# One score tile of four banks for two key chunks, one exponential for both, and the products of a group placed side by side on TensorE

## The chip, the cores and the metric

The kernel runs on one core of one Trainium2 chip. The time is device microseconds of one execution. Of the kernel before, three runs were timed and one further execution was recorded by the hardware profiler. All rows below come from that one.

## What is computed

Routed attention, then a feed-forward block with squared ReLU:

```python
# q, k, v: (4, 8, 768, 64); centroids: (8, 16, 64); w_in: (512, 2048); w_out: (2048, 512)
q_assign = argmax(einsum('bhsd,hcd->bhsc', q_n, c_n), axis=-1)   # nearest of 16 centroids
k_assign = argmax(einsum('bhsd,hcd->bhsc', k_n, c_n), axis=-1)
mask = q_assign[:, :, :, None] == k_assign[:, :, None, :]
scores = where(mask, q @ k.T / sqrt(64), -1e9)
attn = softmax(scores)
x = (attn @ v) as (3072, 512)
h = x @ w_in                                       # (3072, 2048)
out = (maximum(h, 0) ** 2) @ w_out                 # (3072, 512)
```

## The kernel before

**Units.** Two heads make a pair (16 pairs, 4 per batch). The 768 queries of a pair are two halves of 384. The 768 keys are six chunks of 128. The main loop (L481) goes over units `(pair, half, c)` of two key chunks: three units make a half, 96 units in all, numbered from 0. Units 0 to 11 are the first halves of batch 0, units 12 to 23 its second halves, and from unit 24 on both halves of a pair follow each other.

**Scores.** `scores` (L329) handles one chunk. Keys are the stationary operand, so a tile `sc` holds 128 keys by 384 queries for each of the two heads, in one bank per head. Head 0 lies on rows 0 to 63 of the contraction, head 1 on rows 64 to 127, so the products of the two heads use different halves of TensorE's rows. In batch 0 the mask is added by two further products of one-hot codes (L340, "oh"). In the later batches the exponentials are masked on VectorE (L347), by a comparison of the query's and the key's cluster ids. ScalarE takes the exponential of each chunk (L345, 768 elements in each partition). GpSimd adds up the exponentials of a half (`acc`, L357 and L361), except in the first halves of batch 0, where TensorE sums them (`sm`, L374).

**Values.** Two units later (`LAG`), `times_v` (L363) multiplies the exponentials with V: head 0 writes the upper 64 partitions of `av`, head 1 the lower 64, so here the two heads use different halves of TensorE's columns. At the end of a half, `finish` sums `acc` over the partitions with two products (`sm`, L393), takes a reciprocal (`rb`, L397) and writes the scaled result to `xT` (L398).

**Other work on TensorE.** `prep` makes a pair ready: transposes of q and k (`pt`, L229), logits against the centroids (`lg`, L245), their transposes (`lt`, L256). VectorE finds the ids from them (L260 to L281). From batch 1 on six id products in two tiles spread the ids over the partitions (`pb`, L305). A finished batch or half gives FFN work: 64 products `ph` of 384 columns and 48 products `po` of 512 for each half (L416, L429); they are handed out to the units in equal shares as `fill`. On the chip each float32 product of these kinds stands in the trace as two records.

**Start.** The 32 blocks of the weights come in as 64-bit numbers and are rounded, two for each unit: two steps on ScalarE (L131, L133), three on VectorE (L136, L140, L143), one on GpSimd (L147).

**Order.** No order is written out by hand. A list scheduler places the instructions of each engine: of those that are ready by its own estimate it takes the one with the highest priority, and priority falls in the order in which the program is written. Each engine then runs its own list in order. So a score product can be placed alone where its tile is free and its partner's is not, or where something of higher priority is ready in between. PSUM's eight banks are: two tiles of two for scores (`ps_sc`, L71), two for `av` and the first sums, two for all else (`ps_f`). The exponentials have seven tiles of one chunk each (`expp`, L60).

Of the kernel before, what the change touches and what calls it, by code (L numbers as in the profile page):

```python
# [8 lines left out]
F32 = mybir.dt.float32  # L9
# [15 lines left out]
def kernel(  # L25
# [10 lines left out]
    nc = tc.nc  # L36

    B, H, S, D = q.shape
    C = centroids.shape[1]
    NCH = S // P  # L40
# [39 lines left out]
    raw_v = {}  # L80
# [78 lines left out]
    ups = const.tile([P, D], F32, name="ups")  # L159
# [12 lines left out]
    cnT = const.tile([P, H * C], F32, name="cnT")  # L172
# [46 lines left out]
    qkT = {}  # L219
    ids = {}  # L220
    qid = {}
# [19 lines left out]
    def logits(pair):  # L241
        hp = pair % HP
        lg = bank("lg", [P, TB])
        for g in range(4):
            nc.tensor.matmul(  # L245
                lg[32 * g : 32 * g + 32], lhsT=cnT[:, 2 * C * hp : 2 * C * (hp + 1)],
                rhs=qkT[pair][:, NB * g : NB * (g + 1)], start=True, stop=True,
            )
        lgs[pair] = rbp.tile([P, TB], F32, name="lgs", tag="rb")
        nc.scalar.copy(out=lgs[pair], in_=lg)  # L250

# [67 lines left out]
    ex = {}  # L319
    acc = {}  # L320
    sums = {}

    def first_half(pair, h):
        return pair < HP and h == 0

    av = {}
    xT = {}

    def scores(pair, h, c):  # L329
        sc = ps_sc.tile([P, 2, 512], F32, name="sc")  # L330
        for e in range(2):
            rows = slice(D * e, D * (e + 1))
            nc.tensor.matmul(  # L333
                sc[:, e, 0:TB], lhsT=qkT[pair][rows, NCH + c],
                rhs=qkT[pair][rows, NB * h : NB * (h + 1)], start=True, stop=pair >= HP,
            )
        if pair < HP:
            for e in range(2):
                rows = slice(D * e, D * (e + 1))
                nc.tensor.matmul(  # L340
                    sc[:, e, 0:TB], lhsT=qid[pair][1][rows, 1, c * P : (c + 1) * P],
                    rhs=qid[pair][1][rows, 0, h * TB : (h + 1) * TB], start=False, stop=True,
                )
        t = expp.tile([P, 2, TB], F32, name="ex")
        nc.scalar.activation(out=t, in_=sc[:, :, 0:TB], func=ACT.Exp, scale=SCALE)  # L345
        for e in range(0 if pair < HP else 2):
            nc.vector.scalar_tensor_tensor(  # L347
                out=t[:, e], in0=qid[pair][1][:, h, e],
                scalar=ids[pair][:, c % NB, 2 + c // NB, e : e + 1], in1=t[:, e],
                op0=ALU.is_equal, op1=ALU.mult,  # L350
            )
        ex[pair, h, c] = t
        if first_half(pair, h):
            return
        if c == 1:
            acc[pair, h] = accp.tile([P, 2, TB], F32, name="acc")
            nc.gpsimd.tensor_tensor(  # L357
                out=acc[pair, h], in0=ex[pair, h, 0], in1=t, op=ALU.add
            )
        elif c > 1:  # L360
            nc.gpsimd.tensor_tensor(out=acc[pair, h], in0=acc[pair, h], in1=t, op=ALU.add)  # L361

    def times_v(pair, h, c):  # L363
        if c == 0:
            av[pair, h] = ps_av.tile([P, TB], F32, name="av", tag="av")
            if first_half(pair, h):
                sums[pair, h] = ps_av.tile([P, TB], F32, name="sm", tag="av")
        for e in range(2):
            nc.tensor.matmul(  # L369
                av[pair, h][D * e : D * (e + 1)], lhsT=raw_v[pair][:, e, c],  # L370
                rhs=ex[pair, h, c][:, e], start=(c == 0), stop=(c == NCH - 1),
            )
        for e in range(2 if first_half(pair, h) else 0):
            nc.tensor.matmul(  # L374
                sums[pair, h][D * e : D * (e + 1)], lhsT=ups, rhs=ex[pair, h, c][:, e],
                start=(c == 0), stop=(c == NCH - 1),
            )
        if c > 0:
            ex.pop((pair, h, c))
            ex.pop((pair, h, 0), None)  # L380

    def finish(pair, h):
        b, hp = divmod(pair, HP)
        if hp == 0:
            pool = xtp if (2 * b + h) % 3 < 2 else later["xT"]
            xT[b, h] = pool.tile([P, KT, TB], F32, name="xT")
        if first_half(pair, h):
            sm = sums.pop((pair, h))
        else:
            total = acc.pop((pair, h))  # L390
            sm = bank("sm", [P, TB])
            for e in range(2):
                nc.tensor.matmul(  # L393
                    sm[D * e : D * (e + 1)], lhsT=ups, rhs=total[:, e], start=True, stop=True
                )
# [85 lines left out]
    for u in range(len(units) + LAG):  # L481
        if u < len(units):
            pair, h, c = units[u]
            if (p := next_pair(u)) is not None:
                ahead.extend(prep(p))
            if c == 0 and u + 3 < len(units) and units[u + 3][0] not in raw_v:
                load_v(units[u + 3][0])
            for i in range(2):
                scores(pair, h, c + i)
        done = None  # L490
        if u >= LAG:
            pair, h, c = units[u - LAG]
            for i in range(2):
                times_v(pair, h, c + i)
# [241 lines left out]
```

## Time and profile before

| What | us |
|---|---|
| median of three runs (lowest, highest) | 1160.06 (1159.22, 1162.47) |
| profiled execution | 1158.28 |
| its span, first to last instruction | 1156.4 |
| TensorE busy (matmuls) | 1112.3 |
| VectorE busy | 552.3 |
| ScalarE busy | 316.4 |
| GpSimd busy | 312.8 |

How to read it: the span is 1.9 us shorter than the time of the same execution; what lies outside is not in the trace. A busy time is the time in which at least one instruction ran on an engine. Matmuls overlap, so a busy TensorE can still be slowed by the way in which they follow each other. The page also has a chain of waits: from the last instruction back, at each step to what released it. Where it stays on TensorE, its pieces are the net time that each group of matmuls cost, from its start to the start of the next.

### The profile page before, as it was taken

How to read it: one execution, taken by the hardware profiler on the slowest of the kernel's cores; microseconds unless marked ns; L12 is line 12 of the kernel's file. 1: busy time of each engine (PE TensorE's matmuls, PEld its weight loads, DVE VectorE, ACT ScalarE, POOL GpSimd, SP SyncE). 2: the span in 40 equal slices, each digit the busy share in tenths (PEclk: the TensorE clock that was granted, in tenths of full speed). 3: DMA queues.
4: the chain of work that ended last, by engine and by line, in shares of the span. 5: the costliest groups of instructions: out<-in, count | busy, mean ns of one | idle time of the engine just before them, and what ended most of it. 6: DMA issues, size and time to landing. Idle time of an engine off the chain costs nothing.

```text
span 1156.4 us, 10628 instructions
## 1 busy us (share of the span) xinstructions
PE 1112.3 (96%) x4195; PEld 511.6 (44%) x4195; DVE 552.3 (48%) x762; ACT 316.4 (27%) x512; POOL 312.8 (27%) x181
## 2 busy tenths in 40 slices
PE   5987999999999999999999999999999998999997
PEld 3432444444444434544445444544444443554543
DVE  5999222238676665752456533664455641210200
ACT  4765322223332323221223312232122210110110
POOL 2445422214343333331223231331232321000000
PEclk8998999999999999999999999999999999999999
DMA  8864001120110101010100102000000000000000
GB/s 212 257 201 147 15 13 33 31 60 1 41 38 4 50 10 50 1 41 10 45 15 9 34 9 60 1 14 1 18 24 1 1 10 18 1 1 19 9 10 20
DMA packets 63883, 44.32 MB, mean 38 GB/s; under 512 B 51537, under 2 KB 56657, under 8 KB 63825
## 3 DMA queue, kind: packets, MB, share of 16 engines
q1 hardware_dynamic: 63824, 43.56, 13.2%
q8 instruction: 35, 0.57, 0.2%
q14 instruction: 24, 0.19, 0.1%
HBM read 37.26 MB, written 6.29 MB: 38 GB/s over the span
## 4 chain that ended last, share of the span: by engine, by line
PE 88%; DVE 7%; issue 2%; ACT 1%; DMA 1%; SPq 1%; POOL 0%; DVEq 0%; POOLq 0%; ACTq 0%
PE ph L416 30%; PE po L429 29%; PE sc L333 11%; PE av L369 11%; PE sm L393 2%; PE pt L229 2%; DVE w_raw L143 1%; PE pb L305 1%; DVE rb L397 1%; PE lg L245 1%; DVE w_in L136 1%; DVE ids L271 1%; DVE best L266 1%; DVE mx L260 1%; DVE best L262 1%
## 5 line engine op out<-in xcount | busy, mean ns | idle before, releaser
L416 PE MATMUL ph<-xT,w_in 128*128 128x384 f32 x1024 | 353.3, 495 | 0.0
L429 PE MATMUL po<-w_out,gT 128*128 128x512 f32 x768 | 347.9, 599 | 0.0
L361 POOL TENSOR_TENSOR acc<-acc,ex 128x768 f32<-128x768 f32 x112 | 215.0, 1919 | 399.0 <-DVE ex L347 322.7
L347 DVE SCALAR_TENSOR_TENSOR ex<-qid,ids,ex 128x384 f32<-128x384 bf16 x288 | 229.3, 847 | 158.1 <-ACT ex L345 157.8
L416 PEld LDWEIGHTS ph<-xT,w_in 128*128 128x128 f32 x1024 | 188.3, 190 | 153.3 <-issue 26.7
L429 PEld LDWEIGHTS po<-w_out,gT 128*128 128x128 f32 x768 | 139.8, 190 | 174.5 <-issue 171.1
L345 ACT ACTIVATE ex<-sc 128x768 f32<-128x768 f32 x192 | 149.1, 809 | 209.2 <-PE sc L333 153.0
L424 DVE TENSOR_TENSOR gT<-gT 128x384 f32<-128x384 f32 x128 | 91.8, 721 | 221.1 <-ACT gT L423 220.8
L333 PE MATMUL sc<-qkT 64*128 64x384 f32 x768 | 185.2, 518 | 2.1 <-ACT ex L345 2.1
L369 PE MATMUL av<-ex,v_raw 128*64 128x384 f32 x768 | 156.3, 504 | 7.5 <-DVE rb L397 7.5
L423 ACT ACTIVATE gT<-ph 128x384 f32<-128x384 f32 x128 | 62.9, 491 | 290.2 <-PE ph L416 290.2
L397 DVE RECIPROCAL rb<-sm 128x384 f32<-128x384 f32 x32 | 81.7, 2554 | 87.0 <-PE sm L393 81.1
L333 PEld LDWEIGHTS sc<-qkT 64*128 64x128 f32 x768 | 74.0, 188 | 88.3 <-issue 60.1
L357 POOL TENSOR_TENSOR acc<-ex 128x768 f32<-128x768 f32 x28 | 50.7, 1811 | 179.2 <-DVE ex L347 153.2
L369 PEld LDWEIGHTS av<-ex,v_raw 128*64 128x64 f32 x768 | 49.1, 137 | 94.1 <-issue 83.6
L436 ACT COPY osb<-po 128x512 f32<-128x512 f32 x24 | 14.1, 586 | 175.5 <-PE po L429 175.5
L147 POOL TENSOR_TENSOR w_in<-w_in,w_raw 128x512 int32<-128x512 int32 x16 | 22.7, 1418 | 42.6 <-DVE w_raw L143 39.7
L234 ACT COPY qkT<-pt 128x512 f32<-128x512 f32 x32 | 18.7, 584 | 53.4 <-PE pt L229 53.4
L309 ACT CAST qid<-pb 128x384 bf16<-128x384 f32 x48 | 21.9, 480 | 40.2 <-PE pb L305 40.0
L143 DVE SCALAR_TENSOR_TENSOR w_raw<-w_raw 128x512 uint32<-128x512 uint32 x32 | 30.6, 955 | 0.5 <-ACT w_raw L133 0.5
L232 DVE COPY qkT<-pt 128x512 f32<-128x512 f32 x16 | 11.0, 689 | 40.2 <-PE pt L229 40.2
L147 POOL TENSOR_TENSOR w_out<-w_out,w_raw 128x512 int32<-128x512 int32 x16 | 22.3, 1392 | 24.3 <-DVE w_raw L143 17.7
(72 smaller groups left out, 396.1 us busy)
## 6 DMA issues: line engine op xcount, KB each, us to landing
w_raw<-in_moe_w_in_dram SPq DMA_DIRECT2D x16, 512.0 KB, 5.5
w_raw<-in_moe_w_out_dram SPq DMA_DIRECT2D x16, 512.0 KB, 3.5
v_raw<-in_v_dram SPq DMA_DIRECT2D x20, 384.0 KB, 3.3
q_raw<-in_q_dram SPq DMA_DIRECT2D x32, 192.0 KB, 3.8
k_raw<-in_k_dram SPq DMA_DIRECT2D x32, 192.0 KB, 4.0
out_dram<-osb SPq DMA_DIRECT2D x24, 256.0 KB, 2.0
cen<-in_centroids_dram SPq DMA_DIRECT2D x1, 32.0 KB, 1.9
```

Of the source, the lines that this page charges most:

```text
L147: nc.gpsimd.tensor_tensor(out=dst, in0=dst, in1=lo, op=ALU.add)
L333: nc.tensor.matmul(sc[:, e, 0:TB], lhsT=qkT[pair][rows, NCH + c], rhs=qkT[pair][rows, NB * h : NB * (h + 1)], start=True, stop=pair >= HP,)
L345: nc.scalar.activation(out=t, in_=sc[:, :, 0:TB], func=ACT.Exp, scale=SCALE)
L347: nc.vector.scalar_tensor_tensor(out=t[:, e], in0=qid[pair][1][:, h, e], scalar=ids[pair][:, c % NB, 2 + c // NB, e : e + 1], in1=t[:, e], ...
L357: nc.gpsimd.tensor_tensor(out=acc[pair, h], in0=ex[pair, h, 0], in1=t, op=ALU.add)
L361: nc.gpsimd.tensor_tensor(out=acc[pair, h], in0=acc[pair, h], in1=t, op=ALU.add)
L369: nc.tensor.matmul(av[pair, h][D * e : D * (e + 1)], lhsT=raw_v[pair][:, e, c], rhs=ex[pair, h, c][:, e], start=(c == 0), stop=(c == NCH - 1),
L397: nc.vector.reciprocal(out=rb, in_=sm)
L416: nc.tensor.matmul(ph, lhsT=w_in[:, kk, f * P : (f + 1) * P], rhs=xT[b, h][:, kk], start=(kk == 0), stop=(kk == KT - 1),)
L423: nc.scalar.activation(out=gT[f], in_=ph, func=ACT.Relu)
L424: nc.vector.tensor_tensor(out=gT[f], in0=gT[f], in1=gT[f], op=ALU.mult)
L429: nc.tensor.matmul(po, lhsT=gT[f][:, i * P : (i + 1) * P], rhs=w_out[:, f], start=(f == 0), stop=(f == FT - 1),)
```

## The change

- A unit's two chunks go into one tile of four banks, `[P, 2, 2, 512]` (chunk, head, 512). There is one such tile (`ps_sc`, `bufs=1`) where there were two of two banks.
- One exponential covers both chunks: 1536 elements in each partition instead of two of 768. `expp` has three tiles of two chunks instead of seven of one.
- A new helper, `together`, writes the first product of a group at its usual priority and the others at one raised by 2000, so that the scheduler puts them right behind the first. It is used for logits, scores (with the one-hot products behind them), values with the first sums, and the sums of a half.
- The masks and the sums on GpSimd are the same instructions on slices of the new tile.

```diff
-    expp = ctx.enter_context(tc.tile_pool(name="expp", bufs=7))
+    expp = ctx.enter_context(tc.tile_pool(name="expp", bufs=3))
-    ps_sc = ctx.enter_context(tc.tile_pool(name="ps_sc", bufs=2, space=PSUM))
+    ps_sc = ctx.enter_context(tc.tile_pool(name="ps_sc", bufs=1, space=PSUM))
+    def together(products):
+        products = iter(products)
+        nc.tensor.matmul(**next(products))
+        with tc.high_priority(offset=2000):
+            for product in products:
+                nc.tensor.matmul(**product)
 def scores(pair, h, c):
-        sc = ps_sc.tile([P, 2, 512], F32, name="sc")
+        sc = ps_sc.tile([P, 2, 2, 512], F32, name="sc")
+        heads = [(i, e, slice(D * e, D * (e + 1))) for i in range(2) for e in range(2)]
+        products = [
+            dict(
+                out=sc[:, i, e, 0:TB], lhsT=qkT[pair][rows, NCH + c + i],
                 rhs=qkT[pair][rows, NB * h : NB * (h + 1)], start=True, stop=pair >= HP,
             )
+            for i, e, rows in heads
+        ]
         if pair < HP:
+            products += [
+                ...
+            ]
+        together(products)
-        t = expp.tile([P, 2, TB], F32, name="ex")
-        nc.scalar.activation(out=t, in_=sc[:, :, 0:TB], func=ACT.Exp, scale=SCALE)
+        t = expp.tile([P, 4, TB], F32, name="ex")
+        nc.scalar.activation(
+            out=t, in_=sc.rearrange("p i e n -> p (i e) n")[:, :, 0:TB], func=ACT.Exp, scale=SCALE
+        )
 ...
 def times_v(pair, h, c):
-        for e in range(2):
-            nc.tensor.matmul(
-                av[pair, h][D * e : D * (e + 1)], lhsT=raw_v[pair][:, e, c],
-                rhs=ex[pair, h, c][:, e], start=(c == 0), stop=(c == NCH - 1),
-            )
+        for what in ["av", "sums"] if first_half(pair, h) else ["av"]:
+            for i in range(2):
+                for e in range(2):
+                    products.append(dict(
+                        out=(av if what == "av" else sums)[pair, h][D * e : D * (e + 1)],
+                        lhsT=raw_v[pair][:, e, c + i] if what == "av" else ups,
+                        rhs=t[:, 2 * i + e], start=(c + i == 0), stop=(c + i == NCH - 1),
+                    ))
+        together(products)
```

**TensorE, where a pair is routed (the last one, pair 15).** Before, from the transposes of its logits on (`lt`; `sc` scores, `av` values, `pb` id products, `ph` FFN products, `sm` sums; "..." where rows are left out):

```order
L256 MATMUL lt<-ident,lgs 128x128 x3
L333 MATMUL sc<-qkT 128x384 x4
L369 MATMUL av<-ex,v_raw 64x384
...
L416 MATMUL ph<-xT,w_in 128x384 x4
L333 MATMUL sc<-qkT 128x384
...
L305 MATMUL pb<-ident_b,ids_b 128x128
L333 MATMUL sc<-qkT 128x384
L416 MATMUL ph<-xT,w_in 128x384 x5
L333 MATMUL sc<-qkT 128x384 x2
L369 MATMUL av<-ex,v_raw 64x384 x4
```

Here the four score products of a unit stand at three places, and the values of an earlier one are cut by the id products too. After, at the same place (L81 is the first product of a group, L84 are the others):

```order
L266 MATMUL lt<-ident,lgs 128x128 x3
L81 MATMUL sc<-qkT 128x384
L84 MATMUL sc<-qkT 128x384 x3
L81 MATMUL av<-ex,v_raw 64x384
L84 MATMUL av<-ex,v_raw 64x384 x3
...
L315 MATMUL pb<-ident_b,ids_b 128x128
L81 MATMUL sc<-qkT 128x384
L84 MATMUL sc<-qkT 128x384 x3
L435 MATMUL ph<-xT,w_in 128x384 x4
```

Every group is whole, and between two score groups stand four value products and six id products.

**ScalarE, at the end of the rounding of the weights.** Before, from the two steps of the 30th weight to the first ReLU (`gT`); an exponential is half a unit: the two single rows are unit 11, x6 are units 12 to 14:

```order
L131 ACTIVATE w_out<-w_raw 128x512
L133 ACTIVATE w_raw<-w_raw 128x512
L345 ACTIVATE ex<-sc 128x768
L131 ACTIVATE w_out<-w_raw 128x512
L133 ACTIVATE w_raw<-w_raw 128x512
L345 ACTIVATE ex<-sc 128x768
L131 ACTIVATE w_out<-w_raw 128x512
L133 ACTIVATE w_raw<-w_raw 128x512
L345 ACTIVATE ex<-sc 128x768 x6
L423 ACTIVATE gT<-ph 128x384 x2
```

After, an exponential is a whole unit; the first row is unit 10's, x3 are units 11 to 13, and the weights between are the 30th to 32nd:

```order
L360 ACTIVATE ex<-sc 128x1536
L139 ACTIVATE w_out<-w_raw 128x512
L141 ACTIVATE w_raw<-w_raw 128x512
L139 ACTIVATE w_out<-w_raw 128x512
L141 ACTIVATE w_raw<-w_raw 128x512
L139 ACTIVATE w_out<-w_raw 128x512
L141 ACTIVATE w_raw<-w_raw 128x512
L360 ACTIVATE ex<-sc 128x1536 x3
L442 ACTIVATE gT<-ph 128x384
```

Unit 11's exponential has moved behind the last weight's steps, and single ReLUs now stand between the units that follow.

## Rows read from the trace of the kernel before

**Rows 1.** Page, head: span, and each engine's busy time and instructions.
```profile
span 1156.4 us, 10628 instructions
PE 1112.3 (96%) x4195; PEld 511.6 (44%) x4195; DVE 552.3 (48%) x762; ACT 316.4 (27%) x512; POOL 312.8 (27%) x181
```

**Rows 2.** Busy time by stretch: length, five engines (count), granted clock, DMA share, GB/s.
```profile
13.70:111.00 97.30, 77.58 (x429) 35.05 (x430) 90.90 (x133) 63.89 (x101) 42.28 (x31) 0.88 0.70 213
123.30:979.80 856.50, 850.31 (x3226) 382.75 (x3224) 429.19 (x566) 223.81 (x360) 258.24 (x136) 1.00 0.08 21
```

**Rows 3.** Waits of matmuls, 123 to 980 us: total us, times, longest.
```profile
PE pb L305 <- DVE ids_b L281: 6.1, 10, 0.8
```

**Rows 4.** Chain of waits, undisturbed units: start us, net us, what (records).
```profile
879.97 1.49 PE sc L333 x8
881.46 1.44 PE av L369 x8
882.90 6.00 PE ph L416 x18
888.90 0.80 PE sm L393 x4
```

**Rows 5.** Chain of waits where pair 15 is routed.
```profile
863.36 2.78 PE ph L416 x8
866.14 0.84 PE sc L333 x2
866.98 0.44 PE pb L305 x6
867.42 0.84 PE sc L333 x2
868.26 3.42 PE ph L416 x10
871.68 0.85 PE sc L333 x4
```

**Rows 6.** Groups of ScalarE (busy, mean ns | idle), then a timeline of one unit.
```profile
L345 ACT ACTIVATE ex<-sc 128x768 f32<-128x768 f32 x192 | 149.1, 809 | 209.2 <-PE sc L333 153.0 <-PE sc L340 30.0 <-issue 24.6
L309 ACT CAST qid<-pb 128x384 bf16<-128x384 f32 x48 | 21.9, 480 | 40.2 <-PE pb L305 40.0
...
416.93 1.51 ACT L345 ACTIVATE ex<-sc 128x768 f32<-128x768 f32 x2 [0.32 <-PE sc L333]
...
415.92 1.56 PE L333 MATMUL sc<-qkT 64*128 64x384 f32 x8
```

**Rows 7.** Timeline: the last weight's steps on ScalarE and VectorE.
```profile
106.81 0.67 ACT L133 ACTIVATE w_raw<-w_raw 128x512 f32<-128x512 uint32 x1
...
112.86 0.42 DVE L140 TENSOR_SCALAR w_out<-w_out 128x512 uint32<-128x512 uint32 x1
```

**Rows 8.** Chain of waits, end of the start stage.
```profile
97.64 0.68 DVE w_raw L143
...
100.02 0.68 DVE w_raw L143
...
114.61 0.85 PE sc L333 x4
115.46 0.16 PE sc L340 x2
115.62 0.65 PE sc L333 x4
116.26 0.16 PE sc L340 x2
...
119.21 2.57 DVE rb L397
...
129.98 0.84 PE sc L333 x4
```

**Rows 9.** Waits of matmuls for exponentials, whole span: total us, times, longest.
```profile
PE sc L333 <- ACT ex L345: 2.1, 2, 1.1
```

More of the change, by code (lines that the diff above doesn't have):

```diff
@@ L243, in logits @@
         lg = bank("lg", [P, TB])
-        for g in range(4):
-            nc.tensor.matmul(
-                lg[32 * g : 32 * g + 32], lhsT=cnT[:, 2 * C * hp : 2 * C * (hp + 1)],
+        together(
+            dict(
+                out=lg[32 * g : 32 * g + 32], lhsT=cnT[:, 2 * C * hp : 2 * C * (hp + 1)],
                 rhs=qkT[pair][:, NB * g : NB * (g + 1)], start=True, stop=True,
             )
+            for g in range(4)
+        )
         lgs[pair] = rbp.tile([P, TB], F32, name="lgs", tag="rb")
@@ L329, in scores @@
     def scores(pair, h, c):
-        sc = ps_sc.tile([P, 2, 512], F32, name="sc")
-        for e in range(2):
-            rows = slice(D * e, D * (e + 1))
-            nc.tensor.matmul(
-                sc[:, e, 0:TB], lhsT=qkT[pair][rows, NCH + c],
+        sc = ps_sc.tile([P, 2, 2, 512], F32, name="sc")
+        heads = [(i, e, slice(D * e, D * (e + 1))) for i in range(2) for e in range(2)]
+        products = [
+            dict(
+                out=sc[:, i, e, 0:TB], lhsT=qkT[pair][rows, NCH + c + i],
                 rhs=qkT[pair][rows, NB * h : NB * (h + 1)], start=True, stop=pair >= HP,
             )
+            for i, e, rows in heads
+        ]
         if pair < HP:
[L338 to L341, printed above, removed]
+            products += [
+                dict(
+                    out=sc[:, i, e, 0:TB], lhsT=qid[pair][1][rows, 1, (c + i) * P : (c + i + 1) * P],
                     rhs=qid[pair][1][rows, 0, h * TB : (h + 1) * TB], start=False, stop=True,
                 )
-        t = expp.tile([P, 2, TB], F32, name="ex")
-        nc.scalar.activation(out=t, in_=sc[:, :, 0:TB], func=ACT.Exp, scale=SCALE)
[L346 to L350, printed above, removed]
-            )
+                for i, e, rows in heads
+            ]
[3 more added lines that the diff above has]
+            out=t, in_=sc.rearrange("p i e n -> p (i e) n")[:, :, 0:TB], func=ACT.Exp, scale=SCALE
+        )
+        for i in range(0 if pair < HP else 2):
+            for e in range(2):
+                to, ch = t[:, 2 * i + e], c + i
+                nc.vector.scalar_tensor_tensor(
+                    out=to, in0=qid[pair][1][:, h, e],
+                    scalar=ids[pair][:, ch % NB, 2 + ch // NB, e : e + 1], in1=to,
+                    op0=ALU.is_equal, op1=ALU.mult,
+                )
         ex[pair, h, c] = t
@@ L354, in scores @@
             return
-        if c == 1:
+        if c == 0:
             acc[pair, h] = accp.tile([P, 2, TB], F32, name="acc")
+            nc.gpsimd.tensor_tensor(out=acc[pair, h], in0=t[:, 0:2], in1=t[:, 2:4], op=ALU.add)
+        for i in range(2 if c else 0):
             nc.gpsimd.tensor_tensor(
-                out=acc[pair, h], in0=ex[pair, h, 0], in1=t, op=ALU.add
+                out=acc[pair, h], in0=acc[pair, h], in1=t[:, 2 * i : 2 * i + 2], op=ALU.add
             )
-        elif c > 1:
-            nc.gpsimd.tensor_tensor(out=acc[pair, h], in0=acc[pair, h], in1=t, op=ALU.add)
     def times_v(pair, h, c):
@@ L367, in times_v @@
                 sums[pair, h] = ps_av.tile([P, TB], F32, name="sm", tag="av")
-        for e in range(2):
-            nc.tensor.matmul(
-                av[pair, h][D * e : D * (e + 1)], lhsT=raw_v[pair][:, e, c],
-                rhs=ex[pair, h, c][:, e], start=(c == 0), stop=(c == NCH - 1),
[L372 to L380, printed above, removed]
+        t = ex.pop((pair, h, c))
+        products = []
+        for what in ["av", "sums"] if first_half(pair, h) else ["av"]:
+            for i in range(2):
+                for e in range(2):
+                    products.append(dict(
[4 more added lines that the diff above has]
+        together(products)
     def finish(pair, h):
@@ L391, in finish @@
             sm = bank("sm", [P, TB])
-            for e in range(2):
-                nc.tensor.matmul(
-                    sm[D * e : D * (e + 1)], lhsT=ups, rhs=total[:, e], start=True, stop=True
-                )
+            together(
+                dict(
+                    out=sm[D * e : D * (e + 1)], lhsT=ups, rhs=total[:, e], start=True, stop=True
+                )
+                for e in range(2)
+            )
         rb = rbp.tile([P, TB], F32, name="rb")
@@ L487 @@
                 load_v(units[u + 3][0])
-            for i in range(2):
-                scores(pair, h, c + i)
+            scores(pair, h, c)
         done = None
@@ L492 @@
             pair, h, c = units[u - LAG]
-            for i in range(2):
-                times_v(pair, h, c + i)
+            times_v(pair, h, c)
             if c == NCH - 2:
```

## Prediction

> **What bounds the kernel now.** I read the page's head first: TensorE is busy 1112.3 of 1156.4 us [rows 1]. Busy time is an average, so I then split the span into stages [rows 2]. From 13.7 to 111 us TensorE is busy 77.6 of 97.3 us at a granted clock of 0.88, and VectorE 90.9: there the rounding of the weights sets the pace. From 123.3 to 979.8 us TensorE is busy 850.3 of 856.5 us at clock 1.00, and in about that stretch the only wait of a matmul is 6.1 us, in ten pieces, for the routing ids [rows 3]. So this stretch is worth what its instructions on TensorE cost, and a change there has to be priced in TensorE time. From 979.8 us on only FFN products remain, and their order does not change.
>
> What does a product cost there? The chain of waits gives net times, from one start to the next. Undisturbed, a unit of four score products (eight records) takes 1.49 us, four value products 1.44 us, eighteen FFN records 6.00 us and two sums 0.80 us [rows 4]. At a place where a new pair is routed the scores are split [rows 5]: one score product alone (two records) takes 0.84 us, two together (four records) 0.85 us. So the second product of a pair is free when it stands right behind the first, and a lone product costs as much as a pair. The rule that fits all of these: a score group costs 0.21 + 0.645 us per pair begun (0.85, 1.49), a value or sum group 0.16 + 0.645 per pair begun (0.80, 1.44). FFN records: 2.78 us for eight, 3.42 for ten, 6.00 for eighteen [rows 4, 5], which is 0.322 each and 0.20 per group. Each change from one shape of product to another thus costs about 0.2 us, and a broken pair 0.645/2 = 0.32 us.
>
> **The change, part by part.** It adds and removes no product, no mask, no sum and no DMA. It moves products on TensorE, halves the number of exponentials, and leaves one score tile of four banks where there were two of two.
>
> *Steady part.* I count in the order of both programs from the first score product of unit 15 (pair 1, second half, first two chunks) to the tail; the same work is left there in both. Score groups without one-hot products, before: 32 of one product, 9 of two, 9 of three, 53 of four; after: 72 of four. (32 + 9) x 0.85 + (9 + 53) x 1.49 = 127.2 us against 72 x 1.49 = 107.3: 19.9 us less. The groups with one-hot products cost the same in both. Value and sum groups, before: 5 of one, 23 of two, 7 of three, 73 of four, 4 of six; after: 26 of two, 81 of four, 2 of six. 28 x 0.80 + 80 x 1.44 + 4 x 2.09 = 146.0 us against 26 x 0.80 + 81 x 1.44 + 2 x 2.09 = 141.6: 4.4 us less. The remaining groups (FFN, transposes, id products) fall from 135 to 125, at 0.20 us each 2.0 us. Sum: 26.3 us. As TensorE is the path there, all of it counts, unless a wait takes its place.
>
> *The exponential.* Two of 768 elements take 1.51 us back to back, one alone 0.81 [rows 6]. One of 1536 is not in the trace; it lies between 0.81 + 0.70 = 1.51 (nothing saved) and 2 x 0.64 = 1.28 (all fixed cost gone); I take 1.45. ScalarE is not the bound, so the saving is worth nothing by itself; what matters is when it ends, because the one score tile is free only then. A group of eight records that starts at 415.92 ends at 417.48, 0.07 us after the next group has begun [rows 4, 6]. With 0.1 us to start, the exponential ends 0.07 + 0.1 + 1.45 = 1.62 us after the score group has given way, and the next score group may start at about 1.67. In the order of after, no two score groups from unit 12 on stand nearer than 1.44 (four values) + 0.44 (six id products, 0.33 and a change) = 1.88 us, and that at ten places only (at one of them transposes stand for the id products); elsewhere 2.3 us or more. So the cover is 0.2 us at its thinnest. It is gone where ScalarE still has a cast (0.48) in hand [rows 6]: I take 1 us in all, 10 x 0.5 = 5 us as the upper bound, none as the lower.
>
> *Masks, sums on GpSimd, value products.* The masks of a unit start one chunk later and the exp tiles hold three units instead of three and a half. The value products of a unit stand at least 10 us of TensorE work behind its scores from unit 13 on, and the scores of the unit that reuses its tile at least 12 us: more than exponential, masks and sums need. Nothing. The 6.1 us for the ids: between the logits' transposes and the first id product there stood 1.5 to 3.7 us of TensorE work, after the change 2.6 to 3.7. I keep the 6.1 us (bounds: 0 and 6.1).
>
> *Start.* VectorE does the same work, so the rounding ends at about the same time: the last shift ends at 113.28, and ScalarE's last weight step at 107.48 [rows 7]. What changes is the order on ScalarE: the exponential of unit 11 now follows the last weight step; before, both its halves stood ahead of it. It ends at 107.48 + 1.45 = 108.9. Then the last four sums of pair 3, 0.1 + 1.45, to 110.5. Its reciprocal waits for the last shift: 113.28 + 2.57 = 115.9 [rows 7, 8]. Meanwhile TensorE has unit 12's scores 1.81 (0.85 + 0.16 + 0.65 + 0.16 [rows 8]), values 1.44, one FFN product 0.85 and unit 13's scores 1.81, to 116.4, so it need not wait; values 1.44, one FFN product 0.85, unit 14's scores 1.81 and six FFN products 4.07 bring it to 124.6, where unit 15 starts. Before, that was 129.98 [rows 8]: 5.4 us less. Bounds: 10 us less, if the third reciprocal, which now stands ahead of seven weights on VectorE instead of three, lets TensorE go on earlier; 8 us more, if ScalarE comes to its exponentials late.
>
> Sum: 26.3 + 5.4 - 1.0 = 30.7 us. The span goes to 1125.7; the profiled execution, 1158.28 us, to 1127.6; the median of the three runs, 1160.06, which lies 1.8 above it, to 1129.4. Forecast 1129.
>
> **Rivals.**
> *The lone scores were filler.* They stand where a new pair is routed, and if they had covered a wait, removing them only shows it. For: the ten waits for ids are there, after partial filling. Against: the id products come no earlier behind the transposes than before. Price: at each of the 12 places in the steady part the exponential of 1.45 us laid bare once, less the 0.44 us of id products, about 1.0 us: 12 us, to 1141. The Trainium skill, "Perfetto Trace Analysis", section "Matmuls", speaks for this rival: matmul groups should rotate through PSUM banks so that the evacuation of one overlaps the next, and here the rotation falls from two tiles to one. What the trace says against it is the 1.88 us between score groups.
>
> *The start goes in lockstep (slower).* With one tile, TensorE cannot put unit u+1's scores anywhere before the exponential of u, and ScalarE serves that in order between weight steps that wait for DMA and VectorE. TensorE waited for an exponential twice there already, 2.1 us in all, with two tiles [rows 9]. If each of the 12 units of the first half lost an exponential (1.45) and one weight's two steps with the wait ahead of them (2.38 us, the spacing of the weights there, 100.02 - 97.64 [rows 8]), that is 12 x 3.83 = 46 us, and 46 - 26 = 20 us slower: 1180. It decides from 26.3/12 = 2.2 us per unit on. Against: only 2.1 us were lost so far, and TensorE had 20 us to spare in that stage [rows 2].
>
> *The products don't pair as they stand.* If something other than neighbourhood set the pairing (an order of the records, a wait in the group), the lone ones would stay and only the changes saved: 31 score groups, 3 value groups and 10 others, 6.5 + 0.5 + 2.0 = 9 us, to 1151. Against: every undisturbed group of four in the trace is paired [rows 4].
>
> **How the numbers follow.** Forecast near 1129 (1120 to 1137): 0.68. Filler (1137 to 1146): 0.17. No pairing (about 1151): 0.05. Gains eaten by the start, within 3.5 us of 1160 (0.3%, about what a measurement of this kernel can tell from no change): 0.04. Lockstep: 0.06. Low end: 26.3 + 10 + the ids' wait gone would be 42 us, all at once unlikely; I take 40, 1120. High end: 26.3 less 8 at the start and 5 of bare exponentials is 1146, which takes in the filler case. Outside is some 0.16. Faster 0.90, same 0.04, slower 0.06.
>
> **What would show it.** Right: no score group of two records; all at 1.49 us; score groups from unit 12 on 84 instead of 115; unit 15's scores at about 125 us; the tail's last sums end at about 949 us; TensorE's waits for the exponential a few us at most in the steady part. Wrong: a row of waits of TensorE for the exponential with more than 5 us in the steady part, a longer wait for the ids, or unit 15 after 138 us.

## The result, and the profile after

The changed kernel takes 1128.74 us (median of four runs, 1127.61 to 1128.93); the kernel before, in runs on the same chip, 1159.92 us. The ratio is 0.9725, with a 95% interval of 0.9708 to 0.9742: 31 us less. The forecast was 1129 us.

The head of the page after, beside [rows 1] (span; each engine's busy time and instructions):

```profile
span 1125.7 us, 10447 instructions
PE 1084.8 (96%) x4195; PEld 503.9 (45%) x4195; DVE 574.4 (51%) x762; ACT 305.9 (27%) x416; POOL 318.6 (28%) x181
```

TensorE runs the same 4195 records and is busy 27.5 us less; the span is 30.7 us shorter. Busy time by stretch, beside [rows 2] (start and end, length, then PE, PEld, DVE, ACT and POOL with their counts, granted clock, DMA share, GB/s). The second stretch runs from unit 15's scores to the tail, which was 129.98 to 979.78, 849.8 us, before:

```profile
13.70:111.00 97.30, 77.86 (x442) 34.43 (x438) 90.66 (x132) 62.17 (x90) 41.58 (x30) 0.89 0.70 213
127.30:948.76 821.46, 817.57 (x3205) 373.16 (x3204) 450.02 (x562) 214.07 (x277) 264.20 (x136) 1.00 0.08 22
```

So the steady part gave 849.8 - 821.5 = 28.3 us, the start 129.98 - 127.30 = 2.7, and the tail nothing (176.6 us before, 176.9 after). All waits of matmuls in that second stretch (total us, times, longest), beside [rows 3]:

```profile
PE pb L315 <- DVE ids_b L291: 2.4, 5, 0.7
PE pb L315 <- DVE rb L416: 1.2, 2, 0.6
```

No wait for an exponential is among them. The wait for the ids fell from 6.1 us to 2.4. The same id products also waited 1.2 us for a bank that a reciprocal still read, so all waits together are 3.6 us.

Two rows on what the prediction had to guess. The chain of waits at an undisturbed unit (start us, net us, what), beside [rows 4]; L81 is the first product of a group, L84 the others:

```profile
867.61 0.52 PE sc L81
868.13 0.01 PE sc L84
868.14 0.32 PE sc L81
868.45 0.65 PE sc L84 x5
869.10 0.47 PE av L81
...
870.54 6.00 PE ph L435 x18
```

Four score products take 869.10 - 867.61 = 1.49 us, four value products 870.54 - 869.10 = 1.44, eighteen FFN records 6.00, each as before. The group of exponentials on ScalarE, beside [rows 6] (busy us, mean ns | idle before):

```profile
L360 ACT ACTIVATE ex<-sc 128x1536 f32<-128x1536 f32 x96 | 139.2, 1450 | 231.8 <-PE sc L84 231.8
```

It takes 1.45 us.

### The profile page after: what moved, and what is told of

The parts are those of the page before. It is cut to its first block, busy times and chain, and to the rows that moved or that the text cites. A ratio compares the mean times of both kernels' runs of the same rounds, so it can differ in the third digit from the quotient of the medians.

```text
span 1125.7 us, 10447 instructions
## 1 busy us (share of the span) xinstructions
PE 1084.8 (96%) x4195; PEld 503.9 (45%) x4195; DVE 574.4 (51%) x762; ACT 305.9 (27%) x416; POOL 318.6 (28%) x181
## 4 chain that ended last, share of the span: by engine, by line
PE 86%; DVE 7%; issue 3%; DMA 1%; ACT 1%; POOL 1%; SPq 1%; ACTq 0%; POOLq 0%; DVEq 0%
PE po L448 30%; PE ph L435 29%; PE sc L81 6%; PE av L81 5%; PE sc L84 5%; PE av L84 5%; DVE ex L366 2%; PE sm L81 2%; PE pt L237 2%; DVE w_raw L151 1%; DMA w_raw<-in_moe_w_in_dram 1%; DVE rb L416 1%; PE lg L81 1%; PE pb L315 1%; POOL w_out L155 1%
## 5 line engine op out<-in xcount | busy, mean ns | idle before, releaser
L378 POOL TENSOR_TENSOR acc<-acc,ex 128x768 f32<-128x768 f32 x112 | 219.5, 1959 | 416.8 <-DVE ex L366 358.7
L366 DVE SCALAR_TENSOR_TENSOR ex<-qid,ids,ex 128x384 f32<-128x384 bf16 x288 | 246.2, 916 | 154.9 <-ACT ex L360 151.8
L360 ACT ACTIVATE ex<-sc 128x1536 f32<-128x1536 f32 x96 | 139.2, 1450 | 231.8 <-PE sc L84 231.8
L443 DVE TENSOR_TENSOR gT<-gT 128x384 f32<-128x384 f32 x128 | 95.5, 751 | 194.6 <-ACT gT L442 194.2
L84 PE MATMUL sc<-qkT 64*128 64x384 f32 x576 | 151.8, 506 | 0.0
L84 PE MATMUL av<-ex,v_raw 128*64 128x384 f32 x576 | 147.7, 498 | 0.0
L81 PE MATMUL sc<-qkT 64*128 64x384 f32 x192 | 89.2, 545 | 1.7 <-ACT ex L360 1.5
L81 PE MATMUL av<-ex,v_raw 128*64 128x384 f32 x192 | 83.1, 515 | 0.0
L84 PEld LDWEIGHTS sc<-qkT 64*128 64x128 f32 x576 | 66.7, 190 | 26.2 <-issue 2.1
L84 PEld LDWEIGHTS av<-ex,v_raw 128*64 128x64 f32 x576 | 46.6, 137 | 35.4 <-issue 35.1
L81 PEld LDWEIGHTS sc<-qkT 64*128 64x128 f32 x192 | 29.0, 189 | 50.3 <-issue 40.0
L81 PEld LDWEIGHTS av<-ex,v_raw 128*64 128x64 f32 x192 | 18.6, 135 | 44.0 <-issue 43.1
L151 DVE SCALAR_TENSOR_TENSOR w_raw<-w_raw 128x512 uint32<-128x512 uint32 x32 | 36.2, 1130 | 0.1
```

The source lines that it names most:

```text
L81: nc.tensor.matmul(**next(products))
L84: nc.tensor.matmul(**product)
L151: nc.vector.scalar_tensor_tensor(out=lo, in0=hi, scalar=0x80000000, in1=lo, op0=ALU.bitwise_and, op1=ALU.bitwise_or)
L360: nc.scalar.activation(out=t, in_=sc.rearrange("p i e n -> p (i e) n")[:, :, 0:TB], func=ACT.Exp, scale=SCALE)
L366: nc.vector.scalar_tensor_tensor(out=to, in0=qid[pair][1][:, h, e], scalar=ids[pair][:, ch % NB, 2 + ch // NB, e : e + 1], in1=to, op0=ALU ...
L443: nc.vector.tensor_tensor(out=gT[f], in0=gT[f], in1=gT[f], op=ALU.mult)
```

## The experiments

Twelve kernels ran, each beside the kernel before on one chip. The table has the time, its ratio to before (95% interval), the start of unit 15's scores in the trace, and the time from there to unit 95's scores. The last column tells the steady part apart from the start, and is the same 80 units in each. The last two columns come from the one execution of each kernel that was traced.

| Kernel | us | ratio to before | unit 15 at | units 15 to 95 |
|---|---|---|---|---|
| before | 1159.92 | 1 | 130.0 | 819.3 |
| after | 1128.74 | 0.9725 (0.9708 to 0.9742) | 127.3 | 791.1 |
| tile_only | 1169.28 | 1.0074 (1.0057 to 1.0091) | 134.2 | 826.2 |
| place_only | 1129.11 | 0.9737 (0.9718 to 0.9755) | 125.8 | 792.9 |
| two_exps | 1129.11 | 0.9733 (0.9716 to 0.9749) | 128.6 | 790.9 |
| head_order | 1129.22 | 0.9737 (0.9718 to 0.9756) | 127.3 | 791.6 |
| same_half | 1255.31 | one run | 152.5 | 891.5 |
| hold | 1128.37 | 0.9727 (0.9712 to 0.9742) | 129.9 | 789.4 |
| sums_early | 1149.17 | 0.9904 (0.9889 to 0.9919) | 130.0 | 811.3 |
| ahead5 | 1132.87 | 0.9766 (0.9752 to 0.9779) | 132.9 | 791.1 |
| both | 1146.59 | 0.9897 (0.9882 to 0.9913) | 127.3 | 811.1 |
| short_last | 1128.75 | 0.9733 (0.9719 to 0.9746) | 126.9 | 791.5 |
| oht_act | 1129.83 | 0.9733 (0.9718 to 0.9748) | 127.7 | 791.5 |
| oht_short | 1130.02 | 0.9734 (0.9717 to 0.9751) | 129.0 | 791.1 |

Line numbers differ by a few from kernel to kernel; the names in the rows don't.

### Which half of the change: tile_only, place_only, two_exps

tile_only is the change without `together`:

```diff
-        products = iter(products)
-        nc.tensor.matmul(**next(products))
-        with tc.high_priority(offset=2000):
-            for product in products:
-                nc.tensor.matmul(**product)
+        for product in products:
+            nc.tensor.matmul(**product)
```

> The changed kernel with its one tile of four banks and its one exponential, but with every product written at its usual priority. The order on TensorE is then much as before the change: from unit 15's scores to the tail 38 score groups of one product, 8 of two, 9 of three and 52 of four, 76 groups of value and sum products of four, 136 other groups. Theory (the saving is in where the products stand): by the prices 0.21 + 0.645 and 0.16 + 0.645 us per pair begun and 0.20 per other group this is 2.4 us more than before the change, so the gain is gone: 1157 to 1165 us, with lone score products of 0.84 us in the chain. Rival (the one tile or the one exponential brings the gain): 1125 to 1140 us.

It is slower than before by 9 us, above the range that was expected, and the gain is gone. The steady part takes 826.2 us against 819.3, 6.9 more where the prices gave 2.4. Another 3.3 are longer waits: 8.7 us for the ids and 0.7 for a bank, against the 6.1 of [rows 3]. Behind the longest of them (2.5 us) TensorE's granted clock stood at the lower of its two levels, 1.2 GHz: it was 0.51 from 309.1 to 312.6 us, with TensorE busy all the time, which by estimate cost 3.5 x 0.49 = 1.7 us. Four more microseconds went in the start. The lone scores are back in the chain, where pair 15 is routed, as in [rows 5]:

```profile
877.20 0.84 PE sc L81 x2
878.04 0.44 PE pb L312 x6
878.48 0.84 PE sc L81 x2
879.32 3.42 PE ph L432 x10
```

place_only is the other half, `together` on two tiles of two banks:

```diff
-    ps_sc = ctx.enter_context(tc.tile_pool(name="ps_sc", bufs=1, space=PSUM))
+    ps_sc = ctx.enter_context(tc.tile_pool(name="ps_sc", bufs=2, space=PSUM))
...
-        sc = ps_sc.tile([P, 2, 2, 512], F32, name="sc")
+        sc = [ps_sc.tile([P, 2, 512], F32, name="sc") for i in range(2)]
...
-        nc.scalar.activation(
-            out=t, in_=sc.rearrange("p i e n -> p (i e) n")[:, :, 0:TB], func=ACT.Exp, scale=SCALE
-        )
+        for i in range(2):
+            nc.scalar.activation(
+                out=t[:, 2 * i : 2 * i + 2], in_=sc[i][:, :, 0:TB], func=ACT.Exp, scale=SCALE
+            )
```

> The other half alone: products of a group side by side as in the changed kernel, but on two score tiles of two banks, with two exponentials of 768 elements. From unit 15's scores to the tail it has the same 72 score groups of four and 9 with one-hot products as the changed kernel, 109 value and sum groups and 127 others (changed: 109 and 125). Theory (placement alone): the steady part costs within 1 us of the changed kernel's, and the time is 1125 to 1134 us. Rival (the one exponential matters): more than half of the gain is missing, 1145 us or more. Rival (one tile of four banks costs waits that two tiles would not): clearly below the changed kernel's 1128.7 us, 1122 or less.

It has the whole gain. two_exps keeps the one tile and writes the same two exponentials onto it.

> The changed kernel with two exponentials of 768 elements, one after the other, on the one tile of four banks. The groups on TensorE are those of place_only. Theory (ScalarE is not the bound, and the tile comes free only some 0.06 us later): 1125 to 1134 us, no wait of TensorE for an exponential in the steady part. Rival (the length of the exponential is on the path, 96 times 0.06 us and more at the places with the least cover): 1135 us or more.

The three kernels with whole groups lie within 0.4 us of one another, whatever the tile and the exponential. So the gain is in the placement; what the tile and the exponential are worth is too small to tell from nothing here. (In the traces the steady part of place_only is 1.8 us longer than that of the changed kernel, with 5.6 us of waits against 3.6; that of two_exps is 0.2 us shorter.) That also answers the rule the prediction quoted from the Trainium skill, "Perfetto Trace Analysis", section "Matmuls", that groups should rotate through banks: two tiles and one give the same time in this kernel (1129.11 and 1128.74 us).

### What makes two products run side by side: head_order, same_half

The prediction priced a lone product as one without a neighbour of the other head. head_order takes the neighbours away and nothing else:

```diff
-        heads = [(i, e, slice(D * e, D * (e + 1))) for i in range(2) for e in range(2)]
+        heads = [(i, e, slice(D * e, D * (e + 1))) for e in range(2) for i in range(2)]
```

> The changed kernel with the four score products (and the four one-hot products) of a unit in the order head 0, head 0, head 1, head 1 instead of head 0, head 1, head 0, head 1; everything else, on every engine, stands as it did. Theory (two products run side by side only where neighbours use different halves of the rows): of four products only the two in the middle pair, so a group of four costs 0.21 + 3 x 0.645 = 2.15 us instead of 1.50; 81 groups from unit 15 on and three before are 84 x 0.645 = 54 us more, and 12 x 0.16 = 2 us for the one-hot products: about 1185 us (1180 to 1195). Rival (pairing does not go by neighbourhood): 1129 us, groups of four still at 1.5 us.

It cost nothing: my theory fell. The timeline of one score group of head_order (start us, length, engine, line, what):

```profile
400.81 0.59 PE L81 MATMUL sc<-qkT 64*128 64x384 f32 x1
400.83 0.59 PE L84 MATMUL sc<-qkT 64*128 64x384 f32 x1
401.24 0.48 PE L81 MATMUL sc<-qkT 64*128 64x384 f32 x1
401.25 1.13 PE L84 MATMUL sc<-qkT 64*128 64x384 f32 x5
```

And of the changed kernel, its first two rows:

```profile
400.56 0.59 PE L81 MATMUL sc<-qkT 64*128 64x384 f32 x1
400.57 0.59 PE L84 MATMUL sc<-qkT 64*128 64x384 f32 x1
```

In both, a second product starts with the first and not behind its second record, 0.43 us later. In head_order the one written second uses the same rows, so I read the one that starts as the one written third, past it. The gap agrees: the median over all groups after 140 us is 13 ns, against 7 ns in the changed kernel, where one product fewer stands between. The trace doesn't name the rows of a record; this is an inference. The test of it puts all four products on the same rows and so leaves out head 1's scores:

```diff
-        heads = [(i, e, slice(D * e, D * (e + 1))) for i in range(2) for e in range(2)]
+        heads = [(i, e, slice(0, D)) for i in range(2) for e in range(2)]
```

> The changed kernel with the scores of both heads taken from rows 0 to 63 (so head 1's scores are left out and head 0's computed twice); the same products in number, shape and order. The order head 0, head 0, head 1, head 1 had cost nothing, so products do not pair with their neighbour. New theory (each half of TensorE's rows has a line of its own, and a group lasts as long as its fuller half): all four products stand in one line, a group of four costs 0.21 + 4 x 0.645 = 2.79 us instead of 1.50, 84 groups of them 108 us more and 12 with one-hot products 4 us: 1235 to 1260 us. Rival (two products in flight whatever rows they use): 1129 us.

The chain of same_half at one unit:

```profile
525.12 0.84 PE sc L81 x2
525.96 1.94 PE sc L84 x6
```

A group of four takes 2.78 us, where four products one after the other give 0.21 + 4 x 0.645 = 2.79. Here the second product starts only behind both records of the first (749 ns after its start, median of the groups after 140 us). A product on the same rows thus does not start within 13 ns of the first, which bears out the reading of head_order. So each half of the rows does its own products one after the other, and a group lasts as long as the half with the more of them. A lone product is dear, by this account, because the other half has nothing to do until the shape of the products changes. What counts is that both halves get equal work within a group; the order within it doesn't matter. For the groups of the change this gives the same prices, and so the sum held although its reason was wrong.

### Is the hold of the one tile hidden: hold

A second pass over the score tile, which nothing uses, doubles the time for which it is held:

```diff
+        if pair >= HP:
+            held = once.tile([P, 4, TB], BF16, name="held", tag="held")
+            nc.scalar.activation(
+                out=held, in_=sc.rearrange("p i e n -> p (i e) n")[:, :, 0:TB], func=ACT.Exp,
+                scale=SCALE,
+            )
```

> The changed kernel with a second pass of ScalarE over the score tile behind each exponential from unit 24 on (1536 elements, its result is used by nothing), so that the one tile comes free some 1.45 us later. The scheduler knows of the longer hold and moves other work between the score groups: in its order the nearest two score groups stand 3.27 us apart by the prices (1.88 before), more than 1.67 + 1.45 = 3.12; its groups cost 1.6 us less by the prices. Theory (the hold of the one tile is hidden, and would be even at twice its length): 1125 to 1130 us, no wait of TensorE for an exponential in the steady part. Rival (the tile's hold is close to the path everywhere): 72 times up to 1.45 us, 1140 to 1230 us.

The second pass is there, in ScalarE's groups, and all waits of matmuls from 214 to 952 us are still short:

```profile
L365 ACT ACTIVATE held<-sc 128x1536 bf16<-128x1536 f32 x72 | 104.6, 1453 | 0.0
```

```profile
PE pb L315 <- DVE ids_b L291: 2.4, 5, 0.7
PE ph L441 <- DVE rb L422: 0.7, 2, 0.3
```

104.6 us more on ScalarE cost nothing; the steady part is even 1.7 us shorter, where its groups priced 1.6 less. This is no proof for the order of the changed kernel, whose nearest score groups would not cover it: the scheduler moved work between them. It shows that there was enough to move. For the changed kernel's own order the sign is that its steady part has no wait for an exponential.

### Can the prices be used again: sums_early, both

By the prices the two sum products of a half are cheaper in one group with value products:

```diff
             if c == NCH - 2:
                 done = pair, h
+                finish(pair, h)
...
             pair, h = done
-            finish(pair, h)
```

> The changed kernel with the end of a half written right behind its last value products instead of behind the unit's FFN work, so that the two sum products stand in one group with the values in 23 places. From unit 15's scores to the tail: 81 score groups as before, value and sum groups 5 of two, 60 of four and 23 of six instead of 26, 81 and 2, other groups 121 instead of 125. Theory (each change of shape costs about 0.2 us and TensorE is the path): 3.4 + 0.8 = 4.2 us less, 1123 to 1127 us. Rival (the second of the two banks then waits for VectorE's reciprocal of 2.57 us, 23 times): waits of TensorE for the reciprocal take the gain back, 1128 us or more.

The rival was right that a gain in order would be lost in waits, but not in which. It is 20 us slower than the changed kernel. The waits of matmuls from 130 to 971 us:

```profile
PE pb L315 <- DVE ids_b L291: 19.0, 8, 2.7
PE lg L81 <- DVE rb L416: 4.6, 4, 1.3
```

23.6 us in place of 3.6, and 4.2 saved by the order: 15.8 of the 20.2 us by which the steady part grew. Where they come from, in the chain at a place where a pair is routed:

```profile
431.30 1.46 ACT ex L360
432.79 3.75 DVE ex L366 x4
436.54 2.48 DVE rb L416
...
441.14 0.53 DVE mx L270
...
445.03 0.56 DVE ids L281
...
445.84 0.51 PE pb L315 x6
```

The earlier reciprocal stands in VectorE's line ahead of the steps that find the ids (`mx` to `ids`), and the id products wait for them.

The clock fits the rest. After five of these eight waits, each 2.3 to 2.7 us long, TensorE's granted clock fell to the lower of its two levels, 1.2 GHz, and TensorE was busy all through these five stretches. One of them (the columns as in [rows 2]):

```profile
349.50:353.00 3.50, 3.50 (x13) 1.27 (x12) 1.69 (x4) 0.86 (x2) 1.66 (x1) 0.51 0.00 0
```

In the steady part of the changed kernel there is no such stretch. Five times 3.5 us at 0.51 cost, by estimate, 17.5 x 0.49 = 8.6 us. On the other side ten fewer records stand between units 15 and 95 (3107 against 3117), 3.2 us at 0.322 each. Together that is 20.0 + 8.6 - 4.2 - 3.2 = 21.2 us, against 20.2 measured. So a wait of TensorE can cost more than its own length.

both adds a fifth staging buffer (below) to this.

> Five staging buffers and the early sums together. Theory of both: 1128.7 - 2.6 - 4.2 = 1122 us (1120 to 1125). If the fifth buffer is worth nothing, the time of sums_early; if the sums' place is worth nothing, that of ahead5.

It keeps the loss: 811.1 us in the steady part. Its unit 15 starts at 127.3 us, although ahead5, with the same five buffers, comes to 132.9.

### The start: ahead5, short_last, oht_act, oht_short

The start gave 2.7 us where 5.4 was forecast. The 2.7 is read from one execution of each kernel, and executions differ. On every engine hold has the order of the changed kernel up to 214 us, and yet its unit 15 started at 129.9 us, 2.6 later. The stretch from 95 to 105 us, in the changed kernel and in hold:

```profile
95.00:105.00 10.00, 9.80 (x42) 3.46 (x44) 9.97 (x17) 5.42 (x6) 5.00 (x4) 0.83 0.48 157
```

```profile
95.00:105.00 10.00, 8.55 (x24) 2.51 (x26) 8.73 (x15) 3.92 (x5) 3.36 (x3) 0.66 0.30 103
```

The granted clock is the last figure but two: 0.83 and 0.66. In both, TensorE had waited some 2 us for one-hot codes, and its clock stood at the lower level for part of what followed, in hold for longer. In hold VectorE then waited 1.27 us for TensorE's values, and weight steps stood behind that. So a difference of up to some 2.6 us in unit 15 can be that of one execution. By the intervals in the table, only one of the four kernels of this section, ahead5, differs from the changed kernel in time.

The chain of the changed kernel up to unit 15, beside [rows 8]:

```profile
104.21 1.42 POOL w_out L155
105.64 3.39 DMA w_raw<-in_moe_w_out_dram
109.05 0.69 ACT w_out L139
...
110.32 1.34 ACT ex L360
111.71 1.51 PE sm L84 x8
...
127.30 0.52 PE sc L81
```

The last weight's transfer waits for its staging buffer, which GpSimd's add of an earlier weight frees at 105.6; its steps on ScalarE end at 110.3, 2.8 us later than in [rows 7]. So I gave the weights a fifth buffer (and room for it, in tiles that are there anyway):

```diff
-    AHEAD = 4
+    AHEAD = 5
```

> The changed kernel with five staging buffers for the weights instead of four (room is made by keeping the centroids and a few constants of the first microseconds in tiles that are there anyway). TensorE's order is the same, instruction by instruction. Theory (the start gave 2.7 us instead of 5.4 because the last weights' transfers wait for a staging buffer, which GpSimd's adds of weights 24 to 27 gave back late, behind VectorE's reciprocal): with a fifth buffer the last step on ScalarE ends near 107.5 us instead of 110.2, unit 15's scores start at 124 to 125.5 us, and the time is 1125 to 1127.5 us. Rival (TensorE's own work or VectorE's rounding sets unit 15): unit 15 stays at 127.3 +- 0.7 us and the time within 1 us of 1128.7.

It went the other way: unit 15 at 132.9. The fifth buffer let the scheduler put more weight steps ahead of others on VectorE. The chain there:

```profile
99.83 2.47 DVE rb L416
102.30 0.42 DVE ohT L306
...
102.77 0.33 PE sc L84
```

From 102.77 on the chain is TensorE's own work up to unit 15. With so much moved, this run says nothing about the last transfer. short_last leaves every order as it is and makes that transfer short:

```diff
-        nc.sync.dma_start(raw_w[i], weights[i][1])
+        if i == len(weights) - 1:
+            part = NW // 8
+            nc.gpsimd.memset(raw_w[i][:, part:], 0)
+            nc.sync.dma_start(raw_w[i][:, :part], weights[i][1][:, :part])
+        else:
+            nc.sync.dma_start(raw_w[i], weights[i][1])
```

> The changed kernel with the last weight's transfer cut to an eighth of its columns (64 KB instead of 512; GpSimd fills the rest of the staging tile with zeros, so seven eighths of the last weight block are left out). Every other instruction stands in the same order on every engine. Theory (the chain to unit 15 runs from GpSimd's add of weight 27 through the last weight's transfer of 3.39 us, its two steps on ScalarE and the exponential behind them): the transfer takes about 1.8 us, as the smallest one of the page (32 KB), so all behind it comes 1 to 2 us earlier: unit 15's scores at 125.3 to 126.3 us, and the time 1 to 2 us less, 1126.5 to 1128. Rival (VectorE's rounding or TensorE's own work ends at the same time): unit 15 at 127.3 +- 0.4 us, 1128.7.

The transfer fell to 1.8 us, but unit 15 came only 0.4 us earlier. The chain now runs another way:

```profile
92.16 2.46 DVE rb L421
94.62 0.42 DVE ohT L311
...
95.09 0.33 PE sc L84
...
111.34 1.44 PE sm L84 x8
...
126.87 0.52 PE sc L81
```

TensorE waited 2.2 us for the copy of pair 3's one-hot codes (`ohT`), which stood behind the third reciprocal on VectorE, and from then on it had 31.8 us of its own work to unit 15. About 1.6 us of that is the clock: from 95 to 100 us it was 0.67 of full, and the value and one-hot products there took that much longer than the same groups later. So two chains of nearly the same length seem to end there, and in this trace my theory of the last transfer explains 0.4 of 2.7 us. oht_act takes the copy to ScalarE:

```diff
+        elif pair == HP - 1:
+            nc.scalar.activation(out=dst, in_=src, func=ACT.Copy, bias=-BIG, scale=BIG)
```

> The changed kernel with the second copy of pair 3's one-hot codes taken from VectorE to ScalarE, where it stands right behind the first copy instead of behind a reciprocal of 2.5 us. TensorE's order changes in one place: the one-hot products of unit 9 follow its scores at once, where they were cut in three pieces. In short_last TensorE worked without a pause from that copy (95.1 us) to unit 15 (126.9), so this is the chain it should shorten, by the wait of 2.2 us and some 0.8 us for four changes of shape. Theory (two chains of nearly the same length end at unit 15: TensorE's own work since this copy, and the last weight's transfer with its steps): the other chain still ends there, so unit 15 moves by less than 1 us, 126.5 to 127.8. Rival (TensorE's chain alone sets it): 124 to 125 us.

Unit 15 stayed, at 127.7 (two more FFN records, 0.64 us, stand ahead of it there). The wait for the copy is gone and waits for exponentials, which stand among the weight steps on ScalarE, took its place (matmuls, 95 to 130 us):

```profile
PE sm L84 <- ACT ex L362: 2.9, 2, 2.4
PE sc L81 <- ACT ex L362: 2.8, 1, 2.8
```

oht_short, both edits together:

> The last two edits together: the copy on ScalarE, and the last weight's transfer cut to an eighth (seven eighths of the last weight block are left out). In short_last the last weight's steps ended at 109.1 us, with the exponential of unit 11 at 110.6; with TensorE no longer late its last four sums would start then and not at 111.3, and unit 15 some 16 us later. Theory (two chains): unit 15 at 125.5 to 126.3 us, earlier than by either edit alone, and the time about 1 us below the changed kernel's. Rival (neither chain matters, VectorE's rounding does): 127.3 +- 0.4 us.

It missed: 129.0, later than by either edit. TensorE waits for exponentials again, behind weight steps that wait for an earlier transfer:

```profile
PE sc L81 <- ACT ex L367: 2.9, 1, 2.9
PE sm L84 <- ACT ex L367: 2.4, 1, 2.4
```

Behind these waits TensorE's granted clock fell again (0.70 from 105 to 110 us), and a group of scores with its one-hot products took 3.42 us in place of 1.82. These 1.6 us are most of the 1.7 by which unit 15 is later than in the changed kernel. Another execution of the same kernel took 1128.34 us, 2.0 less than the one that was traced. In these traces no single wait holds unit 15 back: take one away, and another within a microsecond or two takes its place. As executions of one order differ by as much, that is not shown beyond them, and which order would bring unit 15 to 124.6 us stays open.

## Why the prediction was right, point by point

- **What bounds the kernel.** Right. The steady part gave 28.3 us. Of these 2.5 are shorter waits for the ids (6.1 to 3.6), and 25.8 are TensorE's own, against 26.3 by the prices. tile_only and place_only show that it comes from the placement.
- **The price of a group.** The numbers held on kernels that the prediction had not seen (2.78 us against 2.79 in same_half). The reason did not: "the second product of a pair is free when it stands right behind the first" is one case of both halves of the rows having work.
- **The exponential.** 1.45 us, as taken; the charge of 1.0 us for ten thin places was not needed, and the lower bound, none, was right. At those places the interval of at least 1.88 us was enough. (The 0.64 us in its lower limit for the exponential stands in none of its rows; the forecast doesn't rest on it.)
- **The ids.** Their waits were kept at 6.1 us. They fell to 2.4; with the new 1.2 us for a bank, 2.5 less in all, inside the bounds.
- **Masks and sums on GpSimd.** Nothing, as said. A mask took 916 ns on average (847 before), off the path.
- **The start.** This step failed: 5.4 us forecast, 2.7 measured. It let the last sums of pair 3 begin at 109.0 us, where they began at 111.7; from them to unit 15 its 15.6 us held. It took ScalarE's last weight step at 107.48 us as before; it ended at 110.3. And it took TensorE as free at 109.0; with the transfer cut short the sums still began only at 111.3, after TensorE's own work, about 1.6 us of it at the lower clock, for which its sum had no term. Both chains pass the third reciprocal, which stands 10 us earlier after the change than before. The timelines of VectorE (start us, length, what), before and after:

```profile
102.39 2.54 DVE L397 RECIPROCAL rb<-sm 128x384 f32<-128x384 f32 x1
```

```profile
92.19 2.54 DVE L416 RECIPROCAL rb<-sm 128x384 f32<-128x384 f32 x1
```

  The text had seen that it moves ahead of more weights, and counted it as a possible gain only; that ScalarE might come late to its exponentials stood in its bounds, without this cause. VectorE had 90.9 of 97.3 us to do in that stage [rows 2], so what is put ahead there makes something else late. How much of the 2.7 us missing is due to this order, and how much to this one execution, stays open.
- **The sum.** 25.8 + 2.5 + 2.7 less 0.3 in the tail is 30.7, the 30.7 that was forecast. To the tenth that is luck: the start gave 2.7 too little, the products 0.5 and the tail 0.3; the ids gave 2.5 and the exponential 1.0 more.
- **The rivals.** "Filler" fell: with the lone scores gone no wait came. "Lockstep" fell: unit 15 came earlier. "The products don't pair as they stand" was right that neighbourhood doesn't set it and wrong in its result, since a whole group gives both halves equal work in any order.

## What to carry to other kernels

Price a group of products by its fuller half of the array plus a fixed cost for each change of shape, read both from the chain of waits, and count groups in the order of the program; that gave 26.3 us where 25.8 were measured. Such a price is a saving only where no other engine's line gets longer by the move: the same prices said 4.2 us for sums_early, and it lost 20, because a reciprocal went ahead of a step that TensorE waits for, and the clock fell behind these waits. In a stage where several engines are nearly full, forecast a moved instruction from both sides, and don't read a microsecond or two out of one execution of it.

## What the runs showed of the hardware

- Products on one half of TensorE's rows can start ahead of one that was written earlier for the other half, still waiting: head_order, 13 ns behind the first where 7 ns are seen in the written order and 749 ns when all are on one half (same_half), and no cost in time (1129.22 us against 1128.74). The Trainium skill, "TensorE: Matmul & The Clock Gate", section "The mechanism", says that matmuls start and end strictly in program order. By that rule head_order would have been some 56 us slower, an estimate from the prices above; here the measurement decides against it, with the reservation that the trace doesn't name a record's rows.
- Four products on one half of the rows take 2.78 us, two on each half 1.49: the halves don't slow each other.
- One exponential of 1536 elements from four banks takes 1.45 us, two of 768 back to back 1.51 [rows 6].
- In sums_early five of eight waits of TensorE, 2.3 to 2.7 us each, were followed by a stretch at the lower of its two clock levels (0.51 from 349.5 to 353.0 us), in which it was busy throughout. In the changed kernel's steady part the clock stayed at 1.00.
